# Loading V of pairs 8, 11 and 14 as a transfer of 120 partitions and one of 8

## The chip, the cores and the metric

The kernel runs on one core of a Trainium2 chip. The metric is the device time of one execution in microseconds (us). Three timed executions of the kernel before gave 413.87, 414.61 and 412.69 us, so the median is 413.87 us. A further execution was profiled.

## What is computed

The reference is one decode step of a gated mix of two blocks, forward and backward. Block A is attention of a single query token over a cache of 32 heads, 4096 positions and 128 features. Block B is a small dense layer with a Mish activation. A scalar gate mixes them. Cut to what matters:

```python
q = (x @ wq).reshape(B, Sq, H, Dh).transpose(0, 2, 1, 3)       # H = 32, Dh = 128, Sq = 1
scores = jnp.einsum("bhqd,bhkd->bhqk", q, k_cache) * (Dh ** -0.5)   # Sk = 4096
p = softmax(scores)
o = jnp.einsum("bhqk,bhkd->bhqd", p, v_cache)
a = o.transpose(0, 2, 1, 3).reshape(B, Sq, H * Dh) @ wo
b = mish(x @ w1 + b1) @ w2
y = g * a + (1 - g) * b                                         # g = sigmoid(sum(x * gate_w))
out, vjp = jax.vjp(f, x, k_cache, v_cache, wq, wo, w1, b1, w2, gate_w)
return (out, *vjp(grad_out))
```

The gradients of the K cache and of the V cache have the size of the caches, 33.6 MB each. So each cache is read once and a gradient of the same size is written once; the page counts 82.03 MB read and 82.03 MB written.

## The kernel before, in words

**Tiling.** The 32 heads are taken in 16 pairs (`NP`, line 58). A pair's K or V is one tile of 128 partitions by 8192 bf16 elements: 64 partitions for each of the two heads, 64 positions in a partition, 16384 bytes a partition, 2 MB a tile. Seven such buffers (`NBUF`, line 67; `bufs`, line 109) serve K and V of all pairs, and one of them first holds the weight w1. The gradient of a tile is written over the tile in place and stored from there, and then the buffer is free for the next load.

**What one pair does.** The sixteen steps of a pair are written out by hand in `slot` (lines 743 to 793). TensorE transposes V and then the next K (`transposes`, line 372), ScalarE copies the transposes out of PSUM (line 379), TensorE multiplies them with do or q (`products`, line 382). Softmax runs on VectorE and ScalarE. `col_sum` (line 430) gives o and dq, and `outer` (line 464) writes the gradient tile as outer products on VectorE, in four quarters. `store_kv` (line 734) then stores the tile.

**Transfers and their order.** All loads stand in one list, `loads` (line 125, filled in lines 161 to 171), in the order K0, V0, w2, K1, V1, w1, K2, V2, and so on. `pump` (line 173) takes from this list as long as a buffer is free, and each load is issued by SP, whose instructions run in order (line 133). A load into a used buffer waits until the store of what was there has wholly landed. Stores of gradient tiles are issued from POOL (line 736) while loads are left, and from SP at the end. So SP's queue (q1) carries mostly loads, and POOL's queue (q0) mostly stores. The output projection wo comes in four groups of eight heads, into two buffers (`ld_wo`, line 158); group 2 and group 3 are loaded into a buffer after the gradient of wo that it held has landed (`plan` with `st_dwo` and `ld_wo`, lines 673, 684 and 686). VectorE needs the new wo for `do_sum` (line 289, instruction on line 290), which is in front of other VectorE work of the pair.

**The end.** After the last pair the gradient of V is stored in two halves (`last_dv`, line 867), the gradient of K in four quarters (`last_dk`, line 872), all from SP; three small results (`fin`, lines 912, 923 and 928) go from ScalarE's queue.

**Completion counts.** In the trace every transfer of SP, ScalarE or POOL has sixteen records of its completion, one for each of the core's 16 DMA engines. A waiting instruction goes on at the sixteenth. The framework gives SP's and ScalarE's transfers eight semaphores in turn, so each transfer also waits until the one eight places before it has landed.

Of the kernel before, what the change touches and what calls it, by code (L numbers as in the profile page):

```python
# [17 lines left out]
def kernel(  # L18
# [33 lines left out]
    nc = tc.nc  # L52
    P = 128
    _, H, Sk, Dh = A_k_cache.shape
# [5 lines left out]
    J = 64  # L60
# [4 lines left out]
    FM = FK * P  # L65
    FN = FK + 1
    NBUF = 7
    NT = 4
    W = 48
    scale = float(Dh) ** -0.5  # L70
# [6 lines left out]
    Vv = A_v_cache.rearrange("b (i h) (p j) d -> (b i) (h p) (j d)", h=2, j=J)  # L77
# [30 lines left out]
    assert R3 <= HC and FN <= 3 * RC and FK % 3 == 1  # L108
    bufs = [big.tile([P, bufw.get(i, KVW)], BF16, name=f"kv{i}", tag=f"kv{i}") for i in range(NBUF)]
    wqa = big.tile([P, RC, H * Dh], BF16, name="wq", tag="wq")  # L110
    wob = [big.tile([P, 8, D], BF16, name=f"wo{i}", tag=f"wo{i}") for i in range(2)]
    tch = [chp.tile([P, 4, P, 2], BF16, name=f"tch{i}", tag=f"tch{i}") for i in range(NT)]

# [8 lines left out]

    free_q = deque(range(NBUF))
    kbuf, vbuf, mbuf = {}, {}, {}
    loads = deque()

    def ld_kv(dct, i, src, pieces, between=None):
        def f():
            b = free_q.popleft()
            dct[i] = b  # L130
            n = J * Dh // pieces
            for t in range(pieces):
                nc.sync.dma_start(bufs[b][:, t * n:(t + 1) * n], src[:, t * n:(t + 1) * n])
                if t == 0 and between:
                    between()
        return (True, f)
# [18 lines left out]
    def ld_wq(c0, c1, eng=nc.sync):  # L155
        eng.dma_start(wqa[:, :, c0:c1], wq_v[:, :, c0:c1])

    def ld_wo(g):
        nc.sync.dma_start(wob[g % 2][:], wo_v[g])
# [4 lines left out]
    for i in range(1, NP):  # L164
        if i == 3:
            loads.append((False, lambda: ld_wq(GC, HC)))
            loads.append((False, lambda: ld_wo(1)))
        loads.append(ld_kv(kbuf, i, Kv[i], 1))
        loads.append(ld_kv(vbuf, i, Vv[i], 1))
        if i == 1:  # L170
            loads.append((True, ld_w1))

# [199 lines left out]
    def transposes(b, c):  # L372
        tp = tr_ps.tile([P, 4, P], F32, name="tr", tag="tr")
        src = fview(b)
        for t in range(4):
            nc.tensor.transpose(tp[:, t, :], src[:, 4 * c + t, :], idf[:])  # L376
        dst = tch[tcount[0] % NT]
        tcount[0] += 1
# [298 lines left out]
    for g in range(NG - 1):  # L677
        i = 4 * g + 4
# [13 lines left out]
    for g in (2, 3):  # L692
        i = 4 * g
# [8 lines left out]
    g, i = NG - 1, NP - 2  # L702
# [156 lines left out]
    i, g = NP - 1, NG - 1  # L859
# [98 lines left out]
```

## Time and profile before

| | us |
|---|---|
| median of three timed executions | 413.87 |
| lowest and highest | 412.69, 414.61 |
| the profiled execution, its own time | 415.07 |
| its span, first to last instruction | 413.3 |
| outside the span | 1.8 |

| engine | busy us | share of the span |
|---|---|---|
| TensorE matmul (PE) | 299.7 | 73% |
| TensorE weight load (PEld) | 273.7 | 66% |
| VectorE (DVE) | 278.7 | 67% |
| ScalarE (ACT) | 264.9 | 64% |
| GpSimd (POOL) | 23.6 | 6% |

The core moved 164.89 MB in 16460 packets, 399 GB/s on average. The mean granted TensorE clock was 0.882 of full speed. An engine's share is a mean over stages with different limits, so the prediction reads stages and not totals: the row of GB/s in 40 slices of 10.3 us, the waits of SP, the chain that ended last, and the sixteen completion records of single transfers.

How those records are read: for a transfer, the times of its sixteen completions are put in order. If the sixteen engines keep step, they lie close together. If the sixteenth stands alone, one engine is behind the others, and all that waits for this transfer waits for that engine.

### The profile page before, as it was taken

To read this page: it belongs to the slowest core of one execution; us is meant where nothing else is said; L and a number is where in the kernel's file an instruction comes from. 1 tells how busy PE (TensorE), PEld (TensorE's weight loads), DVE (VectorE), ACT (ScalarE), POOL (GpSimd) and SP (SyncE) were. 2 spreads that over 40 slices of the span, in tenths; PEclk is the share of its full clock that TensorE was granted. 3 is DMA by queue.
4 is the path that set the end of the run, shared out by engine and by line. 5 is a ranking of instruction groups with operands and counts; after the bars stand their busy time and mean duration, and the time that the engine had idled before them with its cause. 6 is when DMAs were issued, how large, how long until landed. Compare 5 with 4: busy or idle time off the path is not lost.

```text
span 413.3 us, 13115 instructions
## 1 busy us (share of the span) xinstructions
PE 299.7 (73%) x5679; PEld 273.7 (66%) x5682; DVE 278.7 (67%) x602; ACT 264.9 (64%) x537; POOL 23.6 (6%) x47
## 2 busy tenths in 40 slices
PE   3769898997885878649889978209989889786000
PEld 3549888886775778538878878209789788675000
DVE  3647877588775969067995848029795989685900
ACT  3445554799568987246769957016768996995600
POOL 3000100002000101001000101000000100000000
PEclk9879998798999899669999989857999999997555
DMA  8999999999999999999999999999999999999970
GB/s 280 421 410 430 425 414 431 427 408 378 429 425 425 396 425 431 425 430 427 428 428 424 428 429 425 427 432 377 382 387 382 423 427 418 423 426 385 401 254 17
DMA packets 16460, 164.89 MB, mean 399 GB/s; under 512 B 2082, under 2 KB 2274, under 8 KB 6803
## 3 DMA queue, kind: packets, MB, share of 16 engines
q1 hardware_dynamic: 9200, 94.74, 55.7%
q0 software_dynamic: 5376, 63.42, 36.8%
q10 hardware_dynamic: 1826, 5.91, 3.9%
q8 instruction: 44, 0.72, 0.6%
q14 instruction: 14, 0.11, 0.1%
HBM read 82.03 MB, written 82.03 MB: 397 GB/s over the span
## 4 chain that ended last, share of the span: by engine, by line
issue 50%; DMA 19%; PE 11%; DVE 6%; ACT 6%; POOL 3%; SPq 1%; POOLq 0%; ACTq 0%; DVEq 0%
DMA out_dram<-wo 6%; DMA wo<-in_A_wo_dram 5%; DMA kv<-in_A_v_cache_dram 4%; PE tr L376 4%; DMA kv<-in_A_k_cache_dram 3%; DVE kv L467 3%; ACT tch L379 2%; POOL out_dram L736 2%; ACT wo L354 2%; PE dq L435 1%; PE dP L386 1%; PE a_ps L342 1%; PE S L386 1%; DVE wq L488 1%; ACT wq L354 1%
## 5 line engine op out<-in xcount | busy, mean ns | idle before, releaser
L376 PE MATMUL tr<-idf,kv 128*128 128x128 f32 x1024 | 172.3, 295 | 15.7 <-DMA kv<-in_A_k_cache_dram 13.3
L379 ACT COPY tch<-tr 128x512 f32<-128x512 f32 x256 | 144.3, 585 | 56.6 <-PE tr L376 52.2
L376 PEld LDWEIGHTS tr<-idf,kv 128*128 128x128 f32 x1024 | 118.5, 150 | 22.2 <-issue 18.9
L386 PEld LDWEIGHTS <-tch 128*128 128x128 bf16 x2048 | 88.2, 99 | 60.2 <-ACT tch L379 55.9
L467 DVE TENSOR_TENSOR kv<-p_dup,Dr 128x2048 bf16<-128x2048 bf16 x64 | 76.7, 1220 | 6.7 <-ACT p_dup L426 6.3
L467 DVE TENSOR_TENSOR kv<-ds_dup,Qr 128x2048 bf16<-128x2048 bf16 x64 | 76.9, 1219 | 0.4
L386 PE MATMUL S<-qR,tch 128*128 128x48 bf16 x1024 | 48.2, 187 | 35.9 <-ACT tch L379 35.1
L435 PEld LDWEIGHTS <-kv 128*128 128x128 bf16 x2048 | 60.1, 98 | 3.9 <-issue 2.2
L386 PE MATMUL dP<-dR,tch 128*128 128x48 bf16 x1024 | 48.0, 186 | 9.5 <-ACT tch L379 9.2
L290 DVE SCALAR_TENSOR_TENSOR junk<-wo,da_bc 128x640 bf16<-128x640 bf16 x32 | 26.3, 822 | 33.8 <-DMA wo<-in_A_wo_dram 33.1
L426 ACT ACTIVATE p_dup<-e_m,rz 64x128 bf16<-64x128 bf16 x32 | 12.7, 396 | 34.5 <-DVE rz L420 34.0
L435 PE MATMUL dq<-ds_m,kv 128*128 128x48 bf16 x1024 | 31.8, 185 | 2.5 <-DVE ds_m L457 2.5
L354 ACT ACTIVATE wo<-da_bc,o8f 128x640 bf16<-128x640 bf16 (+1 forms) x40 | 32.4, 826 | 1.1 <-PE a_ps L342 0.9
L435 PE MATMUL o<-e_m,kv 128*128 128x48 bf16 x1024 | 32.3, 186 | 0.3 <-issue 0.3
L736 POOL DMA_DIRECT2D out_dram<-kv x25 | 13.4, 536 | 295.6 <-DVE kv L467 285.6
L354 ACT ACTIVATE wq<-dqrow,xf 128x1024 bf16<-128x1024 bf16 (+2 forms) x30 | 24.9, 859 | 1.4 <-DVE wq L488 1.0
L488 DVE SCALAR_TENSOR_TENSOR wq<-wq,dqrow 128x1024 bf16<-128x1024 bf16 (+2 forms) x30 | 25.1, 862 | 0.2
L441 DVE TENSOR_TENSOR o<-o,rz 128x2 f32<-128x2 f32 x16 | 2.5, 158 | 20.8 <-PE o L435 20.8
L408 DVE TENSOR_REDUCE negM<-mt 64x1 f32<-64x64 f32 x32 | 7.1, 222 | 11.3 <-PE mt L405 10.8
L461 ACT COPY ds_dup<-ds_m 64x128 bf16<-64x128 bf16 x32 | 9.5, 297 | 7.3 <-DVE ds_m L457 6.8
L582 DVE SCALAR_TENSOR_TENSOR junk<-wq,db_bc 128x640 bf16<-128x640 bf16 (+1 forms) x14 | 11.5, 821 | 2.2 <-ACT db_bc L258 1.9
L413 ACT ACTIVATE e_m<-S,negM 64x64 bf16<-64x64 f32 x32 | 10.6, 330 | 3.1 <-DVE negM L408 2.6
(156 smaller groups left out, 242.3 us busy)
## 6 DMA issues: line engine op xcount, KB each, us to landing
out_dram<-kv POOLq DMA_DIRECT2D x25, 2048.0 KB, 19.4
kv<-in_A_v_cache_dram SPq DMA_DIRECT2D x16, 2048.0 KB, 18.8
kv<-in_A_k_cache_dram SPq DMA_DIRECT2D x15, 2048.0 KB, 19.2
out_dram<-kv SPq DMA_DIRECT2D x5, 2048.0 KB, 26.3
wo<-in_A_wo_dram SPq DMA_DIRECT2D x4, 1280.0 KB, 19.4
out_dram<-wo POOLq DMA_DIRECT2D x3, 1280.0 KB, 26.5
wq<-in_A_wq_dram SPq DMA_DIRECT2D x2, 1280.0 KB, 9.4
wq<-in_A_wq_dram ACTq DMA_DIRECT2D x1, 2560.0 KB, 43.4
```

What stands on the lines that cost most here:

```text
L290: nc.vector.scalar_tensor_tensor(junk[:], in0=wob[g % 2][:, k, :], scalar=1.0, in1=da_bc[:], op0=ALU.mult, op1=ALU.mult, accum_out=do8[g % ...
L354: nc.scalar.mul(dst, src, col)
L376: nc.tensor.transpose(tp[:, t, :], src[:, 4 * c + t, :], idf[:])
L379: nc.scalar.copy(dst[:].rearrange("p a b e -> p (a b e)").bitcast(F32), tp[:].rearrange("p a b -> p (a b)"))
L386: nc.tensor.matmul(ps[:, 4 * B:4 * B + W].rearrange("p (a b) -> p a b", b=4), lhsT=src[:, t, :, e], rhs=col[:, e, :, :].rearrange("p a b - ...
L413: nc.scalar.activation(e_m[i % 2][HS[hh], :, hh], sview(S_ps[i], hh), ACT.Exp, bias=st[i]["negM"][HS[hh]], scale=1.0, accum_out=rs[i % 2][ ...
L426: nc.scalar.activation(p[HS[hh]], e_m[i % 2][HS[hh], :, hh].unsqueeze(2).to_broadcast([64, J, 2]), ACT.Copy, scale=st[i]["rz"][HS[hh], hh: ...
L435: nc.tensor.matmul(st[i][key][:].rearrange("p (a b) -> p a b", b=2), lhsT=src[:, j, :], rhs=rhs[:, j, :].unsqueeze(1).to_broadcast([P, W / ...
L467: nc.vector.tensor_tensor(kview(b)[:, j0:j0 + n, :].rearrange("p j (a b) -> p j a b", b=2), col[:, j0:j0 + n, :].unsqueeze(2).to_broadcast ...
L488: nc.vector.scalar_tensor_tensor(w, in0=w, scalar=1.0, in1=dqrow[g % 2][:, c0:c1], op0=ALU.mult, op1=ALU.mult, accum_out=dq_acc[:, rc, par ...
L582: nc.vector.scalar_tensor_tensor(junk[0:n, :], in0=w2row(k), scalar=1.0, in1=db_bc[0:n, :], op0=ALU.mult, op1=ALU.mult, accum_out=dact[0:n ...
L736: eng.dma_start(dst, bufs[b][:, 0:J * Dh])
```

## The change

V of pairs 8, 11 and 14 is loaded by two transfers instead of one: the first carries partitions 0 to 119, the second partitions 120 to 127. Both are issued by SP, directly one after the other, into the same buffer. All else stays, the other thirteen loads of V too. The number of instructions of PE, DVE, ACT and POOL is the same; SP issues three more.

```diff
@@ -65,6 +65,8 @@
     NBUF = 7
+    P15 = 120
+    V15 = (8, 11, 14)
@@ -128,7 +130,10 @@
         def f():
             b = free_q.popleft()
             dct[i] = b
-            n = J * Dh // pieces
+            n = J * Dh // max(pieces, 1)
+            if pieces == 0:
+                for r in (slice(0, P15), slice(P15, P)):
+                    nc.sync.dma_start(bufs[b][r, 0:J * Dh], src[r])
             for t in range(pieces):
                 nc.sync.dma_start(bufs[b][:, t * n:(t + 1) * n], src[:, t * n:(t + 1) * n])
@@ -166,7 +171,7 @@
         loads.append(ld_kv(kbuf, i, Kv[i], 1))
-        loads.append(ld_kv(vbuf, i, Vv[i], 1))
+        loads.append(ld_kv(vbuf, i, Vv[i], 0 if i in V15 else 1))
```

## The prediction, as it was put on record

> **What bounds the kernel now.** I read the 40 slices first, then SP's own waits, then windows of the last third, then the chain that ended last, and then the sixteen completion records of single transfers. The page's rows of DMA share and rate:
>
> ```profile
> DMA  8999999999999999999999999999999999999970
> GB/s 280 421 410 430 425 414 431 427 408 378 429 425 425 396 425 431 425 430 427 428 428 424 428 429 425 427 432 377 382 387 382 423 427 418 423 426 385 401 254 17
> ```
>
> The transfers run at some 427 GB/s wherever they have work, that is 26.7 GB/s for each of 16 engines. They fall short of it in slices 28 to 31 (279 to 320 us, 377 to 387) and at the end. SP's waits say who holds the loads back:
>
> ```profile
> SPq L133 <- DMA out_dram<-kv: 284.9, 26, 22.3
> ```
>
> SP waits 284.9 us in all for stores of gradient tiles to land, since a buffer is reloaded only then. The windows show both places where the rest stands still:
>
> ```profile
> 270.00:280.00 10.00, 0.70 (x10) 0.70 (x11) 3.25 (x9) 2.11 (x4) 0.00 (x0) 0.50 1.01 433
> 280.00:290.00 10.00, 9.68 (x164) 9.01 (x166) 9.90 (x16) 6.82 (x14) 0.53 (x1) 0.75 0.91 365
> 390.00:400.00 10.00, 0.56 (x2) 0.50 (x2) 1.94 (x11) 0.00 (x0) 0.53 (x1) 0.50 0.98 338
> 400.00:413.00 13.00, 0.00 (x0) 0.00 (x0) 0.00 (x0) 0.00 (x0) 0.00 (x0) 0.50 0.13 30
> ```
>
> The columns are PE, PEld, DVE, ACT and POOL busy, the clock, DMA share and GB/s. From 270 to 280 PE works 0.70 us of 10 while DMA is full. After that PE is busy 9.68 of 10 and DMA is short of work: there compute sets the pace. After 400 no engine computes, and DMA is 13% busy: a few of its engines end the kernel. The chain of waits names the first place:
>
> ```profile
> 257.58 19.08 DMA wo<-in_A_wo_dram
> 276.69 0.83 DVE junk L290 x2
> ```
>
> VectorE stands until the load of wo, group 3, has landed at 276.66.
>
> **One engine is late.** Of the sixteen completions of that load of wo, the first is at 270.33, the fifteenth at 274.74 and the last at 276.66: 1.92 us alone. For V12 (issued 275.81) the last two are at 288.02 and 294.08; for the store issued at 306.74, 314.57 and 320.99; for the first half of the last dV (380.42), 390.21 and 401.27; for the last quarter of dK (389.90), 406.10 and 412.08. From 285 on one engine is mostly 3 to 11 us behind the other fifteen, in both queues, and its last landing, 412.08, ends the span of 413.3.
>
> **The change, part by part.** Three loads are split.
>
> *The late engine's share.* A tile is 128 rows of 16384 bytes, the trace shows packets of 16384, and so an engine carries 8 packets of a load: 131072 B at 26.7 GB/s is 4.91 us. By the packets' own records, 611 ns each (most common) and the next starting 607 ns later, it is 8 x 0.607 = 4.86 us. Take 4.86. 120 rows are 15 x 8: if an engine keeps 8, fifteen carry the first transfer and the sixteenth carries nothing. The 8 rows left are then one packet each for eight engines, 0.61 us. No row of before shows a transfer of 120 or of 8 partitions, so how they are dealt out is open. Bounds for the late engine, per load: it loses 4.86 us, or, if it isn't the one left out, it gains 0.61 us. I take the loss, because with 15 equal shares some engine goes free, and a single one is late. Over three loads that is 14.58 us, more than its greatest lag, 401.27 - 390.21 = 11.06. The late engine stops being the last; what counts from there is the fifteenth.
>
> [...]
>
> *The stall for wo.* V8 (issued 188.02) and V11 (249.47) stand ahead of that load of wo (257.58) in SP's queue. With either of them off the late engine, wo lands with the fifteenth: 276.66 - 274.74 = 1.92 us earlier. From 276.69 to 391.75 the chain is compute but for one load of K, so compute and the stores that it issues come 1.92 us earlier. That is taken once; SP's shorter waits from 285 to 345 (K15 was issued at 332.98 for a store whose fifteenth landing was 327.44) I put at nothing, because PE is 8.6 to 9.7 us busy in each 10 there: compute covers them. If that cover is thinner than it looks, up to 332.84 - 327.44 = 5.4 us more is gained.
>
> *The end.* The last quarter of dK lands with the fifteenth engine: 412.08 - 406.10 = 5.98 us. What is late next is the last piece of dwq, which lands at 406.20 and whose fifteenth is at 403.26.
>
> *What is added.* Three issues on SP at 0.33 us (the timeline's loads from line 133) fall into the waits above: nothing, and without this cover 1.0 us. Transposes of the split V wait for two landings; the second comes one packet, 0.61 us, behind the first on eight engines, but V11's last landing was 1.90 us behind its fifteenth (268.72, 266.82), so it is still earlier than now. The semaphores move on by one to three places: at the end the half store of the gradient of wo (issued 365.29) then waits for the store of dwq that lands at 366.39, 1.1 us, and behind it on SP stands the store issued at 368.62, which is not reached. One more packet of V14 on a then last engine: +0.61 us, counted whole. Those of V8 and V11 fall before 320, where the fifteen have idle time.
>
> *Sum.* -5.98 - 1.92 + 0.61 = -7.29 us. The profiled execution took 415.07: 407.78. Against the median of 413.87, 1.20 below it, that is **406.6 us**. Ends of this case: all 14.58 us are worth something, 399.3; only V14's share counts and one packet is added, -4.86 + 0.61 = -4.25, 409.6.
>
> **The rivals.**
>
> *A. The late engine is not relieved.* The free engine is another, or the 8 rows go back to the sixteenth. Then the late engine has three more packets, 3 x 0.61 = 1.83 us, or the same as now: 413.9 to 415.7. For it: nothing in the trace tells the engines apart by number. Against it: only that one in sixteen is left out and one is late for a lasting reason. [...]
>
> *B. Fifteen engines collide; slower.* In a load of 128 rows all packets keep 611 ns while no other queue is active. Another dealing of rows can make two engines hinder each other. The nearest row for a packet that shares is 1199 ns, where an engine serves both queues. Price: 8 x (1.199 - 0.611) = 4.70 us for a load, 14.1 us for three, on all fifteen. It outweighs the gain from 7.29 of 14.1 us, about half of the packets; whole, the time is 413.87 - 7.29 + 14.1 = 420.7. For it: the trace has no load that is dealt out in another way. Against it: while the three loads run, stores run in the other queue, and packets take 1199 ns anyway. [...]
>
> *C. Relieved, but hidden.* The late engine is freed, and the end stays with something else: ScalarE's three small results, issued at 394.98, 401.34 and 406.92, each waiting for a semaphore of an earlier store. For it: the third is issued only at 406.92. Against it: these waits end with the late engine's landings (394.90 and 401.27), so they go too. The time would be 412 to 413.9. [...]
>
> **How the numbers follow.** Forecast 0.66; A 0.12; B 0.16; C 0.06. About 0.5% is what a measurement of this kernel can tell from no change, 2.07 us: below 411.8 is faster, above 415.9 slower. The forecast is faster as a whole, 0.66. A ends at 415.7, just within the bound; I leave 0.02 of it for a lag that grows on its way and put 0.10 within. With C's 0.06 that is 0.16 for the same. Slower is B with the 0.02: 0.18. The range takes the forecast with its ends, C and A, 0.84: 399.3 to 415.8. The likeliest case's own range is 399.3 to 409.6.
>
> **What would show it.** In the profile after, the three split loads have completions that lie close, with no sixteenth alone; the load of wo, group 3, lands within 1 us of its fifteenth engine; the last quarter of dK lands near its fifteenth; the windows after 400 us hold almost no DMA. It is wrong if one engine is still 3 us or more alone in the stores after 340 (A), if packets of 16384 B of the split loads take far over 611 ns with the store queue idle or SP's loads land later than now (B), or if these records close up and the span stays (C).

## The result, and the profile after

The change makes the kernel slower. The median of four executions of the changed kernel is 426.62 us (424.9 to 427.34), that of four executions of the kernel before, on the same chip, 414.24 us. The ratio is 1.029, with a 95% interval of 1.026 to 1.033. The forecast was 406.6 us, within 399.3 to 415.8. Rival B, the one that named a collision between engines, had 420.7 us; rival A, that the late engine isn't relieved, 413.9 to 415.7. What both named was then seen: the packets of a load cut by rows take 1212 ns instead of 611 (e1), and one engine is still behind the others (6.0 us in the half store issued at 392.1). In the medians given below for e8 and e10, one execution of each is left out because it was over 1.5% longer than the fastest (427.85 and 457.23 us).

The profiled execution took 424.9 us, its span is 423.1 us, 9.8 us more than before's 413.3. Its page, span, DMA rows and one queue:

```profile
span 423.1 us, 13128 instructions
...
DMA  8999999989999999999999999999979999999991
GB/s 278 422 405 431 430 410 425 429 342 400 427 428 412 400 426 424 430 426 414 383 417 424 424 422 374 394 421 373 395 283 369 369 381 418 422 426 418 387 302 28
...
q1 hardware_dynamic: 9221, 94.74, 55.9%
```

The transfers are almost as busy as before (the row of digits is nearly all nines), but the rates beside them fall where a split load runs. Counted from 0, slice 19 (201 to 212 us) has 383 GB/s, slices 24 and 25 (254 to 275) 374 and 394. A busy share near 100% with a lower rate means that single packets take longer (667 to 687 ns on average in the stretches below, against 614 to 620 before), not that the engines have nothing to do. The lowest rate, 283 in slice 29 (307 to 317), lies where no split load runs, and there the share is down as well, to 7 tenths. Two profiles also differ without the change: from 30 to 190 us, ahead of all three splits, before moved 420 GB/s and after 416, which is 1.5 us of the engines' time. The queue's count of packets tells how the rows were dealt out: 9221 against 9200 before. A load of 128 rows has 128 packets of data and 16 of completion (4 bytes each: before has 1618 of them and as many completion records). The two parts have together the same data packets (7852 of 16384 bytes in both traces), and three loads add 21, seven each, so the two parts have 23 completion packets: fifteen engines for 120 rows and eight for 8 rows. That much of the prediction held. The counts of e1 and e6 fit the same dealing. In e1, 11943 packets of SP's queue less 10112 of data leave 1831, which is the sum of 16 for each of 90 transfers of 16, 32, 64, 96, 112 or 128 rows, 15 for each of 17 of 120 rows and 8 for each of 17 of 8 rows.

The same three stretches in both kernels, first before, then after. The columns are busy time of PE, PEld, DVE, ACT and POOL, the clock, the DMA share and GB/s. In the changed kernel V8 runs in the first stretch, V11 in the second, V14 in the third:

```profile
190.00:215.00 25.00, 21.86 (x404) 19.39 (x403) 21.84 (x46) 18.04 (x40) 1.07 (x2) 1.00 1.01 428
252.00:278.00 26.00, 8.23 (x171) 7.60 (x167) 5.59 (x12) 6.01 (x14) 0.53 (x1) 0.74 1.01 429
330.00:350.00 20.00, 18.08 (x385) 17.00 (x383) 18.02 (x35) 16.24 (x32) 0.85 (x1) 1.00 1.01 425
```

```profile
190.00:215.00 25.00, 19.27 (x360) 17.15 (x359) 21.23 (x43) 16.90 (x37) 1.06 (x2) 0.99 1.01 395
252.00:278.00 26.00, 14.35 (x290) 13.55 (x287) 9.23 (x14) 9.21 (x20) 1.07 (x2) 0.83 1.00 392
330.00:350.00 20.00, 17.61 (x359) 15.78 (x354) 17.96 (x32) 19.70 (x39) 1.06 (x2) 1.00 1.02 377
```

The DMA share is full in all six rows. The rate falls by 33, 37 and 48 GB/s. Over the stretches that is 0.83, 0.96 and 0.96 MB that did not move, or at 427 GB/s 1.9, 2.3 and 2.2 us of the time of all engines: 6.4 us in all, of the 9.8 that the span is longer. The packets say the same: those of 16384 bytes take 667, 673 and 687 ns on average in these stretches, and 614 to 620 ns before.

Who feels it is read from the chain of waits and from SP's waits. The chain of after, at the load of wo, group 3:

```profile
261.40 25.21 DMA wo<-in_A_wo_dram
286.64 0.83 DVE junk L295 x2
```

VectorE waited till 276.69 before, and now till 286.64: 9.95 us later, close to the span's 9.8 us. That the one makes the other does not follow: in e2, below, the same wait ends 6.4 us later than before and the span is not longer. Behind the late wait the transfers are short of work for a while. The same window in before and in after:

```profile
300.00:310.00 10.00, 8.86 (x178) 8.37 (x177) 9.81 (x20) 6.45 (x15) 0.53 (x1) 1.00 0.98 385
300.00:310.00 10.00, 9.49 (x176) 8.51 (x174) 7.99 (x23) 7.39 (x21) 0.53 (x1) 1.00 0.78 325
```

From 290 to 320, with no split load in it, after moved 1.5 MB less than before, 3.6 us of all engines. But e2 moved 1.3 MB less in this stretch too, and ended on time, so how much of it reaches the end isn't shown. SP's waits for a buffer to be stored stay about what they were (257.8 us and, for the split loads that have a line of their own now, 32.9; before 284.9):

```profile
SPq L138 <- DMA out_dram<-kv: 257.8, 23, 23.3
SPq L136 <- DMA out_dram<-kv: 32.9, 3, 13.8
```

The last windows of after, same columns:

```profile
270.00:280.00 10.00, 0.00 (x0) 0.00 (x0) 0.00 (x0) 0.00 (x0) 0.00 (x0) 0.64 0.99 412
280.00:290.00 10.00, 0.75 (x10) 0.75 (x11) 3.30 (x9) 2.16 (x4) 0.00 (x0) 0.50 0.97 409
400.00:410.00 10.00, 0.56 (x2) 0.50 (x2) 3.64 (x13) 1.12 (x3) 0.82 (x1) 0.50 1.00 342
410.00:423.00 13.00, 0.00 (x0) 0.00 (x0) 0.00 (x0) 0.00 (x0) 0.00 (x0) 0.50 0.27 68
```

From 270 to 280 no engine computes at all. The tail of before, in which a few DMA engines finish alone, is still there: 27% busy from 410 on. The prediction had said that these windows would hold almost no DMA.

The completion records of V11's two parts show both failures at once. The first record of each comes half a us after the issue, 14.5 and 15.9 us before the next. The parts of the three loads have six such records, and the trace has six records more than packets of completion (1645 and 1639), so no packet belongs to them; we read them as the count for the engines that have no part. The others are engines, in order of time:

```
V11, 120 rows, issued 252.0:  252.48 | 266.99 ... (13 engines to 271.99) ... 274.18 275.95
V11, 8 rows,   issued 252.4:  252.89 | 268.83 271.12 271.34 272.25 272.98 273.76 276.11 278.12
```

The 8 rows were counted at one packet, 0.61 us behind the 120. Their last landing is 2.2 us behind here, 2.3 us for V8 (214.92 and 212.65) and 3.2 us for V14 (350.24 and 347.08). A late engine remains: in the half store issued at 392.1, the fifteenth engine lands at 401.94 and the sixteenth at 407.94.

One engine is free earlier as well, and it is not the late one. In the transfers behind a split load one engine is now far ahead of all others (up to 12.4 us), while the last is still alone at the end. We take the one ahead for the one that was left out. The store issued at about 250 us in before and at 254.75 in after (first, second, fifteenth and last landing):

```
before  267.34  267.43 ... 273.11  275.67
after   262.12  272.64 ... 279.06  281.06
```

### The profile page after: what moved, and what is told of

It reads as the page before. It is cut to its first block, busy times and chain, and to the rows that moved or that the text cites. A ratio compares the mean times of both kernels' runs of the same rounds, so it can differ in the third digit from the quotient of the medians.

```text
span 423.1 us, 13128 instructions
## 1 busy us (share of the span) xinstructions
PE 305.9 (72%) x5679; PEld 280.7 (66%) x5682; DVE 278.7 (66%) x602; ACT 265.5 (63%) x537; POOL 23.6 (6%) x47
## 3 DMA queue, kind: packets, MB, share of 16 engines
q1 hardware_dynamic: 9221, 94.74, 55.9%
## 4 chain that ended last, share of the span: by engine, by line
DMA 35%; issue 27%; PE 15%; DVE 9%; ACT 6%; POOL 2%; SPq 0%; POOLq 0%; ACTq 0%; DVEq 0%
DMA kv<-in_A_k_cache_dram 16%; DMA out_dram<-kv 7%; PE tr L381 7%; DMA wo<-in_A_wo_dram 6%; DMA kv<-in_A_v_cache_dram 6%; DVE kv L472 5%; ACT tch L384 3%; PE dP L391 2%; ACT wo L359 2%; PE a_ps L347 1%; POOL out_dram L741 1%; PE o L440 1%; DVE wq L493 1%; PE S L391 1%; PE dq L440 1%
## 5 line engine op out<-in xcount | busy, mean ns | idle before, releaser
L381 PE MATMUL tr<-idf,kv 128*128 128x128 f32 x1024 | 178.6, 303 | 23.0 <-DMA kv<-in_A_k_cache_dram 16.6
L381 PEld LDWEIGHTS tr<-idf,kv 128*128 128x128 f32 x1024 | 122.8, 155 | 29.3 <-issue 25.5
L391 PEld LDWEIGHTS <-tch 128*128 128x128 bf16 x2048 | 91.0, 101 | 58.3 <-ACT tch L384 53.4
L391 PE MATMUL dP<-dR,tch 128*128 128x48 bf16 x1024 | 49.1, 188 | 9.7 <-ACT tch L384 9.6
L413 DVE TENSOR_REDUCE negM<-mt 64x1 f32<-64x64 f32 x32 | 7.1, 222 | 13.0 <-PE mt L410 12.4
## 6 DMA issues: line engine op xcount, KB each, us to landing
wo<-in_A_wo_dram SPq DMA_DIRECT2D x4, 1280.0 KB, 15.9
```

The lines of the kernel that those rows point to most:

```text
L391: nc.tensor.matmul(ps[:, 4 * B:4 * B + W].rearrange("p (a b) -> p a b", b=4), lhsT=src[:, t, :, e], rhs=col[:, e, :, :].rearrange("p a b - ...
```

## The experiments

The runs went to the chip in four groups, each with its own executions of the kernel before beside it: medians of 414.18 (e1 to e4), 414.13 (e5 to e8), 415.48 (e9, e10) and 414.35 us (e11, e12). "The late engine" is the one whose record is the last and alone.

### e1: loads by themselves

A kernel with transfers only: loads on SP's queue, groups of six tiles, each group cut in another way, then groups of five beside stores on POOL's queue.

```diff
+    def rows(b, src, *cuts):
+        c = (0,) + cuts + (P,)
+        for x, y in zip(c, c[1:]):
+            nc.sync.dma_start(bufs[b][x:y, :], src[x:y])
...
```

> Leaves out the whole computation: it only loads 2 MB tiles, six in a row in each of nine groups, and stores tiles in five more. Groups: 128 rows; 120+8; 120 alone; 112+16; 64+64; 96+32; two column halves of 128 rows; 8 rows alone; 128 rows; then, beside four stores of 2 MB from POOL, five loads each of 128, 120+8, 112+16, 64+64 and 128 rows. Theory D (dealing: rows dealt out in another way than those of 128 make engines hinder each other): 128 rows and column halves take 6 x 4.9 = 29 us with packets of 611 ns; 120+8, 120 alone, 112+16, 64+64 and 96+32 all take longer packets, 800 to 1200 ns on the mean, 38 to 58 us. Theory S (the second transfer costs: it stands behind the first on eight engines): 120+8 takes 29 + 6 x 0.61 = 33 us with packets of 611 ns, 120 alone 29 us, 112+16 and 64+64 29 us. Theory F (fifteen engines instead of sixteen cost): 120 alone and 120+8 are longer, 112+16, 64+64 and 96+32 as 128 rows, 29 us.

The windows of this kernel, one row for each group: POOL busy, the clock, the DMA share, GB/s. In order: 128 rows; 120 and 8; 120 alone; 112 and 16; 64 and 64; 96 and 32; two column halves.

```profile
0.70:33.10 32.40, 0.00 (x0) 1.00 0.93 388
33.10:104.00 70.90, 0.00 (x0) 1.00 0.88 177
104.00:164.40 60.40, 0.00 (x0) 1.00 0.90 195
164.40:220.50 56.10, 0.00 (x0) 1.00 0.96 224
220.50:282.50 62.00, 0.00 (x0) 1.00 0.97 203
282.50:340.10 57.60, 0.00 (x0) 1.00 0.96 218
340.10:373.10 33.00, 0.00 (x0) 1.00 0.93 382
```

Read the last two columns together: the engines are 88 to 97% busy in every group, and move about half as much as soon as the tile is cut by rows. Cut by columns it costs hardly anything (382 against 388 GB/s). A packet takes 611 ns (median) in a tile of 128 rows, and on average 1212 ns in 120 rows, 1295 in 120 and 8, 1119 in 112 and 16, 1244 in 64 and 64, 1152 in 96 and 32. Eight rows alone, partitions 0 to 7, take 2407 ns each (median). So, by themselves, the second transfer isn't one packet of 0.61 us but one of 2.4 us, and the first isn't 8 x 0.607 = 4.86 us but about 8 x 1.21 = 9.7 us. The later groups have stores on POOL's queue beside them. Two stretches in which both queues work, first with loads of 128 rows, then of 120 and 8:

```profile
400.00:440.00 40.00, 0.00 (x0) 1.00 1.01 425
473.00:503.00 30.00, 0.00 (x0) 1.00 0.97 368
```

In the first, the packets of both queues take 611 ns (median of each); in the second, those of the loads take 702 ns on average and those of the stores 685. So beside stores the loss is 13% instead of about half: a part is hidden, not all, and the stores pay with the loads. Loads of 112 and 16 rows and of 64 and 64 rows come to 364 and 362 GB/s there.

### e2: two column halves

```diff
-                for r in (slice(0, P15), slice(P15, P)):
-                    nc.sync.dma_start(bufs[b][r, 0:J * Dh], src[r])
+                for r in (slice(0, J * Dh // 2), slice(J * Dh // 2, J * Dh)):
+                    nc.sync.dma_start(bufs[b][:, r], src[:, r])
```

> V of the same three pairs in two transfers, but each of 128 partitions by half the columns. Theory D: rows are dealt as before, so the time is that of the kernel before, 414 us, within 2 us. Theory S (two transfers and two landings cost): near the changed kernel, 420 to 427 us. Theory F: as before, 414 us.

Measured: 414.44 us, ratio 1.000 (0.997 to 1.003). The same three loads, in two transfers each, with the same added issues and the same shift of the semaphores, cost nothing that can be measured. It is the cut by rows, not the number of transfers. Its chain at the load of wo, group 3:

```profile
259.08 24.02 DMA wo<-in_A_wo_dram
283.12 0.83 DVE junk L295 x2
```

VectorE goes on at 283.12, 6.4 us later than in before, and the span is 412.3 us, against before's 413.3. A delay of that size at this wait doesn't reach the end.

### e3: the 120 rows alone

```diff
-                for r in (slice(0, P15), slice(P15, P)):
+                for r in (slice(0, P15),):
```

> The changed kernel without its second transfers: partitions 120 to 127 of V of pairs 8, 11 and 14 are not loaded and hold what the buffer held. Theory D: the long packets stay, and so does most of the loss, 419 to 425 us. Theory S: the loss is gone, and with one engine freed the time is at or under that of before, 405 to 414 us. Theory F: the loss stays whole, 426 us.

Measured: 421.52 us, ratio 1.016 (1.011 to 1.021). The first transfers alone cost some 7 us, though they move 0.39 MB less; the second transfers cost the other 5 us of the 12.

### e4 and e8: other places to cut

```diff
-    P15 = 120
+    P15 = 112      # e4; 64 in e8
```

> The split at partition 112 instead of 120: both transfers divide by 16, so all engines take part, with 7 rows and 1 row each. Theory D: blocks of 7 rows are dealt in another way than those of 128 too, packets lengthen, and the time is 420 to 428 us. Theory F: all sixteen engines work, so the time is that of before, 414 us. Theory S: the second transfer stands behind the first on all engines with the same sum of packets, so the time is 414 to 418 us.

> The split at partition 64: all sixteen engines, 4 rows each, twice. Alone, six loads took 62.0 us against 70.9 for 120+8 and 56.1 for 112+16. Theory P: the loss follows that order, so it lies between 420.5 (112+16) and 426.6 (120+8): 421 to 426 us. Rival K or F (few rows, or fifteen engines): two large halves on all engines cost nothing, 414 us.

Measured: 112 and 16 rows 420.53 us, ratio 1.014 (1.007 to 1.021); 64 and 64 rows 419.40 us, ratio 1.012 (1.004 to 1.019). Both use all sixteen engines in both parts (16 completion packets for each part of 112, 16 or 64 rows fit e1's count) and are still slower. Having every engine at work isn't enough. The order of the two was expected to follow e1's rates (224 and 203 GB/s). But 64 and 64 rows lie under the 421 to 426 us expected, and the intervals don't tell the two apart, so that part is not confirmed.

### e5: which engine is late

Tiny transfers of 1 to 8 rows are put ahead of four V loads of the kernel before. In the records below a transfer of 1 to 6 rows has as many landings as rows, so we take n rows to run on n engines.

```diff
+PROBE = {12: (1, 2), 13: (4, 6), 14: (3, 5), 15: (7, 8)}
...
+            nc.sync.dma_start(pt[i, k][0:k, :], x_v[0:k])
...
```

> The kernel before with eight tiny extra loads of 10 bytes a row from SP, of 1 and 2, 4 and 6, 3 and 5, 7 and 8 rows, ahead of V of pairs 12, 13, 14 and 15. The completions in the changed kernel fit n rows on n engines, so each goes to a known set. Theory: the late engine isn't the one that 120 rows leave out, but among the eight of the 8-row transfers. Then the 8-row probe's last completion stands alone by 2 us or more as that of the V load behind it does, and the probes with fewer rows show from which number on. If the late engine is the left out one, no probe shows a lag and the V loads still do. The eight loads cost 8 x 0.33 us on SP and up to 3 us.

Measured: 413.57 us for the one execution, so the probes hardly disturb. Their records without the first, early one, and the fifteenth and the last landing of a full load that was issued shortly ahead:

```
1 row:  279.99      2 rows: 280.16 281.87               full load: 283.74, 286.75
4 rows: 299.78 300.02 300.24 300.78                     full load: 304.64, 307.11
6 rows: 301.01 301.28 301.49 302.05 305.84 308.49
3 rows: 322.25 322.35 323.20                            full load: 324.85, 329.00
5 rows: 322.33 323.82 323.90 324.74 330.64
7 rows: last 352.79    8 rows: last 353.46              full load: 346.36, 352.31
```

The late engine is in the sets of 5, 6, 7 and 8, and not in those of 1 to 4. If these sets lie within each other, and if it is the same engine at 300 us (where 4 and 6 rows were sent) and at 320 us (3 and 5 rows), it is the fifth. No run here shows which engines make up a set, so this stays an assumption. If it is also in the set that the 8 rows of a split load use, and has its share of the 120 rows, it carries eight packets of the 120 rows and one of the 8 rows. It is then given more work, not less, which fits the lone last record in both parts of V11 above (1.8 and 2.0 us behind the one before it).

### e6: which rows hinder each other

Groups of six loads or stores by themselves, 8 or 16 rows on as many engines or whole tiles, the rows placed in different ways. The page's 1114 packets of completion fit that: 16 for each of 22 transfers of 128 rows and of 18 of 16 rows, 15 for each of 6 of 120, 8 for each of 48 of 8.

```diff
+    def load(last, d, s):
+        order = [last] + [x for x in range(6) if x != last]
+        for b in order:
+            nc.sync.dma_start(bufs[b][d, :], Kv[n[0] % NP][s])
+    e = load(e, slice(0, 8), slice(0, 8))
+    e = load(e, slice(0, 32, 4), slice(0, 8))
+    e = load(e, slice(0, 8), slice(0, 32, 4))
...
```

> Leaves out the whole computation: groups of six transfers with nothing beside them: 128 rows; 8 rows at partitions 0 to 7; at 0, 4, 8 .. 28; at 0 to 7 from HBM rows four apart; at 0, 2 .. 14; at 0, 16 .. 112; at 120 to 127; 16 rows at 0 to 15; at 0, 4 .. 60; at 0, 8 .. 120; 128 rows; then stores of 128, 120 rows, 8 rows from 0 to 7 and from 0, 4 .. 28. Theory P (engines that write neighbouring partitions share a port of the buffer memory, four neighbours and the four 32 further on have one): packets take 611 ns for 128 rows and for 8 rows four apart, 2 x 611 = 1222 ns for 8 rows two or sixteen apart and for 16 rows four or eight apart, 4 x 611 = 2444 ns for 8 or 16 neighbours, also with HBM rows four apart. Rival H (neighbouring rows in HBM hinder each other): 2400 ns wherever the HBM rows are neighbours, 611 ns with HBM rows four apart. Rival K (a transfer of few rows is slow by itself): all groups of 8 and 16 rows alike. Stores: under P the same factors if reading shares the port too.

The windows of this kernel, columns as in e1. In order, loads into: partitions 0 to 7; 0, 4 to 28; 0 to 7 again, from rows of HBM that lie four apart; 0, 2 to 14; the sixteen 0, 4 to 60. The last two rows are stores from 0 to 7 and from 0, 4 to 28:

```profile
33.00:48.70 15.70, 0.00 (x0) 1.00 0.42 50
48.70:56.10 7.40, 0.00 (x0) 1.00 0.29 106
56.10:71.80 15.70, 0.00 (x0) 1.00 0.42 50
71.80:81.70 9.90, 0.00 (x0) 1.00 0.37 79
119.50:129.10 9.60, 0.00 (x0) 1.00 0.69 164
261.40:277.90 16.50, 0.00 (x0) 1.00 0.46 48
285.90:291.70 5.80, 0.00 (x0) 1.00 0.32 136
```

Eight engines move the same bytes in 15.7 us or in 7.4 us, by the place of the partitions alone; where the rows lie in HBM changes nothing (15.7 us both times). The packets:

| partitions of the load | packet, median ns | engines that share a group |
|---|---|---|
| all 128 | 611 | not counted |
| 0 to 7 | 2400 | 4 |
| 0, 4 to 28 | 611 | 1 |
| 0 to 7, HBM rows four apart | 2407 | 4 |
| 0, 2 to 14 | 1273 | 2 |
| 0 to 15 | 2407 | 4 |
| 0, 4 to 60 | 1276 | 2 |
| 0, 8 to 120 | 1284 | 2 |

The last column is counted by theory P's grouping, with one row on each engine: four neighbouring partitions and the four that lie 32 further are one group. The packets take 611 ns with one engine in a group, 1273 to 1284 with two, 2400 to 2407 with four, so every row that could be counted agrees with it. That four neighbours count is seen from 0 to 7, 0, 2 to 14 and 0, 4 to 28 (2400, 1273 and 611 ns). The rows 0, 4 to 60 and 0, 8 to 120 (1276 and 1284 ns) need partitions further apart to meet as well; "32 further" fits both, and no single pair was tried. What the engines of a group share, a port or something else, no run shows, nor which of the 128 rows of a whole tile an engine gets. Stores behave alike: 2533 ns from 0 to 7, 615 ns from 0, 4 to 28. Two further groups overlapped in time and are left out.

### e7, e9, e11, e12: one split at a time

```diff
-    V15 = (8, 11, 14)
+    V15 = (14,)     # e7; (8,) in e9; (11,) in e11; (10,) in e12
```

> The change for V of pair 14 alone. Theory P: each split costs its long packets by itself; the compute of the changed kernel was set back by 3.4 us after V8, 4.9 after V11 and 2 after V14, so 416 us, 414 to 418. If the first split only shifts the order of things and all else follows from that: 414 us, as before. If V14's split relieves the end as forecast: 408 us.

> The change for V of pair 8 alone. Theory P (shared ports make the packets long; each split costs by itself): compute in the changed kernel was set back by 3.4 us after V8, so 415 to 419 us. If only the end counts, and a split before the last third is made up for: 414 us. If V8's split frees the late engine, which the probe puts at number five of sixteen and not at the left out one: 412 us or less.

> The change for V of pair 11 alone. The three splits together cost 12.4 us, V8 alone 2.0 and V14 alone 2.9 us at the middle of their ratios. If the costs add up, V11 has the rest, 7.5 us: 421 to 424 us at a kernel before of 415, because V11 stands directly ahead of the load of wo for which VectorE stands still. If each split alone costs 2 to 3 us and they make each other worse: 417 to 418 us.

> The same for V of pair 10 alone, which has two more loads between it and the load of wo. If the place ahead of wo is what makes V11 dear, V10 costs as V8, 2 us: 416 to 418 us. If the costs grow with the time at which a split stands, V10 lies between V8 and V14: 417 to 418 us, and V11 too.

| split | us | ratio | 95% interval | us more |
|---|---|---|---|---|
| V8 (e9) | 417.50 | 1.005 | 1.002 to 1.008 | 2.0 |
| V11 (e11) | 417.93 | 1.008 | 1.005 to 1.011 | 3.4 |
| V14 (e7) | 417.57 | 1.007 | 1.005 to 1.010 | 2.9 |
| V10 (e12) | 418.07 | 1.008 | 1.005 to 1.011 | 3.4 |

("us more" is the ratio's excess times the kernel before.) The loss is made where the split is. The windows of e11, same columns as the first windows above, show the rate down in the second stretch alone:

```profile
190.00:215.00 25.00, 21.83 (x406) 19.33 (x404) 21.82 (x47) 17.73 (x41) 1.06 (x2) 1.00 1.01 429
252.00:278.00 26.00, 9.61 (x168) 8.87 (x166) 3.84 (x8) 5.75 (x13) 0.53 (x1) 0.74 1.00 381
330.00:350.00 20.00, 17.75 (x367) 16.30 (x366) 18.61 (x33) 18.28 (x35) 0.84 (x2) 1.00 1.01 425
```

What fell is the expectation for e11: V8 and V14 left some 7 us of the 12 for V11, and its place right ahead of the wait for wo was to explain why it costs more. It costs 3.4 us, as V10 does.

### e10: eleven splits

```diff
-    V15 = (8, 11, 14)
+    V15 = tuple(range(5, 16))
```

> The same split for V of pairs 5 to 15, eleven instead of three. Theory P: the price grows with the number, 11 x 2.95 us (V14 alone) to 11 x 4.1 us (a third of the changed kernel's loss): 447 to 460 us. If the loss comes from one bad meeting in the last third and not from each split: under 435 us.

Measured: 453.19 us, ratio 1.088 (1.081 to 1.096), about 3.3 us for each split. The lines of its page:

```profile
span 451.7 us, 13155 instructions
...
GB/s 277 422 418 428 418 420 424 425 350 390 362 366 424 359 369 429 370 399 369 395 377 393 393 383 381 414 291 233 376 208 380 365 358 390 325 356 415 340 295 114
```

From slice 10 on, where V5 is loaded (113 us), the rate is under 420 in all but two slices. A split costs about as much among eleven as by itself, so nothing of a relieved late engine shows in their sum either.

## Why the prediction was wrong

**"If an engine keeps 8, fifteen carry the first transfer ... a single one is late": the dealing was right, the engine was wrong.** Fifteen engines and then eight, as the counts show. But the late engine isn't the one left out: after has one engine up to 12.4 us ahead of all others, and another one still behind. I had reasoned that "with 15 equal shares some engine goes free, and a single one is late", which are two facts about two engines; nothing joined them. The text itself said that nothing in the trace tells the engines apart by number, and gave that case 0.12. So the terms -5.98 us (the end) and -1.92 us (wo, group 3) did not come. In their place the load of wo still ends 2.6 us behind its fifteenth engine (284.01, 286.61), the half store at 392.1 us 6.0 us and the last quarter of dK 3.0 us (419.08, 422.10).

**The packets were kept at 607 to 611 ns, and the second transfer "one packet, 0.61 us, behind": these terms were mis-sized.** Alone, a packet of the 120 rows takes 1212 ns and one of the 8 rows 2407 ns (e1). Rival B had the mechanism and a price of 4.70 us for a load; the loads alone give 8 x (1.212 - 0.611) = 4.8 us. In the kernel a part is hidden while the engines' other queue works, as in e1 beside stores: 1.9 to 2.3 us of all engines' time for each split by the windows, 2.0 to 3.4 us by the single splits. Why a second queue hides it wasn't tried. The term +0.61 us for "one more packet" stands against some 5 us for the three second transfers (e3 against the whole change).

**Why B had only 0.16.** Against it I held that packets take 1199 ns anyway while the store queue runs. That was misread. In the three stretches of before, both queues are at work and move 425 to 429 GB/s, and the packets of each take 611 ns (median), as they do in e1. Of 7808 packets of 16384 bytes in before ten took 1199 ns, eight of them close together at 290 us. So the two queues share an engine without longer packets, and the argument against B was none. B's price was worked out from the same 1199 ns; that it came near the 1212 ns of e1 is luck. For another dealing of rows there was a row to read, though not a clear one: in before, the two halves of the gradient of wo, group 3, are stored from 64 partitions each. Their packets of 10240 bytes take 577 and 696 ns on average (medians 387.5 and 629.5), against a median of 385 ns in the loads of wo with 128 partitions. I called the trace empty of other dealings, and these were there.

**"DMA is short of work: there compute sets the pace", from 280 to 320 us: misread too.** The DMA share there is 0.91 to 1.02 at 365 to 392 GB/s, and the packets of 16384 bytes take 666 ns on average, against 615 from 190 to 280. The engines were mostly busy with longer packets, the same sign as in after. What made them longer in before wasn't tried.

**Rival C, relieved but hidden: it had no relief to hide.** The late engine is still 6.0 us behind in the half store at 392.1 us. Nor did the time stay: the runs show a loss of 1.2 to 2.9% for the cuts by rows.

**"Three issues on SP ... nothing" and the semaphores: right.** e2 has the same issues and the same shift and measures 1.000 (0.997 to 1.003).

**The stall for wo: the wrong sign, and the path behind it isn't there.** The prediction counted 1.92 us at the wait for wo, group 3, as 1.92 us at the end, since from there "the chain is compute". The wait ended 9.95 us later instead. And e2, whose wait ends 6.4 us later at an unchanged time, shows that a shift at this wait doesn't carry to the end one for one. The loss is better told by what the engines moved less.

**What stays open.** The three single splits add up to 2.0 + 3.4 + 2.9 = 8.3 us; all three together cost 12.1 us (10.6 to 13.6 by the interval). The rest, about 3.8 us, is more than these intervals explain when they are combined as independent errors (some 2.5 us). The 3.6 us that the engines moved less between 290 and 320 us would fit it, but e2 has nearly the same lack there and no loss, so whether delays of one split make the next one dearer wasn't settled. Why one engine is late in the kernel before wasn't tried. No version was found that is faster than the kernel before: each cut by rows that was tried costs time, and the cut by columns leaves each engine its share.

## What to carry to other kernels

Cut a tile's transfer by columns, not into blocks of neighbouring partitions, when the DMA engines are the bound: the same three loads in two pieces cost nothing by columns and 1.2 to 2.9% by rows. Before relying on an engine that is "left out", find out which one is late; tiny transfers of 1 to 8 rows narrowed it down in one run and hardly disturbed the kernel. A wait that ends later isn't yet a longer kernel: e2's ended 6.4 us later for nothing. And when a rival needs a price for another way of dealing rows, look for any transfer in the trace that has fewer partitions, and compare its packets with those of the same size from 128. Take the price from the median of many packets; the 1199 ns of ten packets were no rule.

## What the runs showed of the hardware

- A packet of 16384 bytes takes 611 ns when its engine is alone in its group of partitions, counted as in e6, 1273 to 1284 ns with two engines there, 2400 to 2407 ns with four. That is 2.1 and 3.9 times as long, and the DMA share counts the longer packets as busy (0.88 to 0.97 in e1's cut groups).
- A tile cut into 64 and 64 rows runs at 203 GB/s and 128 rows at 388 GB/s (e1), with all sixteen engines in both by e1's count of packets; a packet takes 1244 ns on average in the one and 611 ns (median) in the other.
- 120 rows reach all groups of partitions, counted as in e6, and still run at 195 GB/s, with packets of 1212 ns on average (e1). So how many groups a transfer reaches doesn't tell its rate. That it depends on which engines are in the same group at the same time was my reading, from e6's 611 to 2407 ns; no run shows which rows an engine gets. The price of the cuts by rows was 1119 to 1295 ns a packet (averages of e1's cut groups) against 611.
- Two queues with work on the same engines don't lengthen packets by themselves: 611 ns (median) in each queue at 425 GB/s in e1 and at 425 to 429 GB/s in three stretches of before.
